# Delta-rule attention, Fourier MLP and token mixing in one Trainium2 kernel: another written-out order of the instruction queues

## The chip, the cores and the metric

One core of one Trainium2 chip runs the whole program. The metric is the device time of an execution in microseconds (us); smaller is better. The kernel before took 953.66 us (median of 3 runs, 952.69 to 954.89).

## The reference

Three steps, each fed by the one before, in float32. A delta-rule attention over 4 batches, 8 heads, 768 positions of width 48; an MLP with a two-dimensional Fourier transform ahead of it; and a token mix with three more weight matrices.

```python
k_n = k / (np.linalg.norm(k, axis=-1, keepdims=True) + 1e-06)
for t in range(S):                                   # attention, state is (B, H, 48, 48)
    y[:, :, t] = einsum('bhd,bhde->bhe', q[:, :, t], state)
    v_old = einsum('bhde,bhd->bhe', state, k_n[:, :, t])
    state = state + beta[:, :, t] * einsum('bhd,bhe->bhde', k_n[:, :, t], v[:, :, t] - v_old)

X = np.fft.fft(np.fft.fft(x, axis=1), axis=2)        # x is y with the heads side by side: (4, 768, 384)
u = x + np.real(X)
un = (u - mean(u)) / np.sqrt(var(u) + 1e-06)
x = u + np.maximum(un @ w_ch1, 0.0) @ w_ch2          # 384 -> 1536 -> 384

theta = x @ w_theta
y = einsum('ts,bsd->btd', w_tok_r, x * cos(theta)) + einsum('ts,bsd->btd', w_tok_i, x * sin(theta))
u = x + y
out = u + np.maximum(u @ w_ch, 0.0)
```

## The kernel before

**Attention.** The 768 positions are cut into 12 windows of 64 per batch; all 48 (4 batches of 12) are scanned in turn. Two windows make a chunk step d (24 of them, 16 pairs of head and window each), and four steps share a solve, T0 to T5. `gram` (L351 to L386) loads keys and queries with the DMA kt, multiplies them on TensorE (PE) into sm and copies the products to KQ. `solve` (L397 to L438) inverts 128 triangular 32x32 blocks on VectorE (DVE): 30 pairs of a product (L434, tmp) and a sum (L437, T), the first pair and the last of 30 elements and the middle ones of 240. `solved` transposes the result twice, into TN (L446) and TT (L448). `chunks` (L509 to L537) makes pa from TN, A on ScalarE (ACT, L518), pt from A and TT, copies TT and pt into YU (L483 or L485, L531), multiplies into pw and copies that to YU (L537). `load` (L493, L495) brings the tiles YQ and Y. `scan` (L549 to L584) is the serial chain from window to window: pu (PE), X (ACT, L555 and L556), ps (PE), X of the next window (ACT, L566 and L567), and py (PE); after every second window a tile y is copied out of py (L581, L583) and stored to ysc (L584). YQ, Y and X have two buffers each, so a load of step d waits until the scans of step d-2 have read them.

**Weights.** They come as 64-bit floats. `Split.steps` turns 128x384 numbers at a time into a high and a low part: a DMA into a raw tile (L239), the magnitude on ACT (L242), the sign on DVE (L243), three more steps there (L244 to L246), the low bits (L249), the high part on ACT (L250), three matmuls that add the pieces up (L251 to L253) and a copy on ACT (L254). There are two raw tiles, so the DMA of one conversion waits for L249 of the last but one. w1 and w2 of the MLP need 24 such conversions, which stand among the attention of batch 0 and 1; those of the token mix (wth, wtr, wti) begin when the last scan has been issued and the attention's buffers are given back.

**Fourier and MLP.** `fourier_inputs` (L610 to L656) folds the six y of a batch with sums and differences on DVE or GpSimd (POOL), two scalings on ACT (L626, L631) among them; `fourier_1` (L671) and `prepare` (L747 to L791) transform and normalise (un, L760); `ffn_up` (L204 to L206, ph; then hh on ACT L802 and hl on DVE L803) and `ffn_down` (L812 to L815, pc) are the MLP. Every product of it is three matmuls, of high and low parts. Then the token mix follows (L1056 to L1136).

**What sets the order.** The Python code writes the instructions down step by step (the string PLAN sets how attention and weights mix). `arrange` then reads the table ORDER: for PE, ACT, DVE and POOL it holds runs "skip+n" over the engine's written instructions (go on by skip, take n), and it chains the instructions in the order so read, so that each of these four queues is fixed to the last instruction. SyncE (SP), which issues nearly all DMAs, is not in the table: the scheduler places its DMAs by what they wait for. The innermost lines:

```python
        for run in runs.split():
            skip, n = run.split("+") if "+" in run else (run, 1)
            at += int(skip)
            queue += w[at:at + int(n)]
            at += int(n)
        for a, b in zip(queue, queue[1:]):
            tc.add_manual_dep(b, a.name, edge, reason="order")
```

Of the kernel before, what the change touches and what calls it, by code (L numbers as in the profile page):

```python
# [80 lines left out]
    "PE": """32+32 -64+32 32+179 111+16 -127+16 56+6 -62+16 70+3 -73+16 162+16 -178+8 49+6 16+16 83+16 -186+16 6+8 8+8 -16+8  # L81
# [46 lines left out]
 63+18 -81+18 27+18 18+18 -81+9 72+63""",  # L128
    "Activation": """0 6+6 -12+2 1+3 -4 9+2 24 -25+2 23 -24+2 46 -25 24 -48+3 46 -47+4 52 -10 -44+13 3 38 -3 -37+2 1 -2 1+2 40+4
# [1130 lines left out]
```

## Time and profile before

| | us |
|---|---|
| median of 3 runs (lowest to highest) | 953.66 (952.69 to 954.89) |
| the profiled execution: its own time | 952.9 |
| its span, first to last instruction | 951.1 |
| PE busy | 877.6 |
| DVE busy | 647.8 |
| ACT busy | 431.3 |
| POOL busy | 304.7 |

The span is what the trace covers; the execution's own time holds 1.8 us more around it. An engine's busy time is the sum over its instructions. The granted clock of TensorE is given as a share of full speed: 0.50 is the lower of its two levels, 1.00 the upper; its mean over the span was 0.930. Names in the rows leave buffer numbers out: w_384ag is w1_0_384ag as well as w1_2_384ag.

### The profile page before, as it was taken

The numbers are of one execution on the slowest core, as the hardware profiler recorded it, in microseconds if no ns is written. First come the engines' busy times: TensorE is split into PE (matmuls) and PEld (weight loads), VectorE is DVE, ScalarE is ACT, GpSimd is POOL, SyncE is SP. The second block draws the span as 40 slices with busy tenths as digits, with TensorE's granted clock in tenths as the row PEclk, the third lists the DMA queues.
The fourth block names the chain that finished last, engine by engine and source line by source line (L and its number), as shares of the span: only waits on it lengthen the run. The fifth ranks groups of instructions, "written<-read, shape, count | busy, mean of one in ns | idle before, by whom it ended". The sixth has DMA issues, their size and how long they took to land.

```text
span 951.1 us, 23435 instructions
## 1 busy us (share of the span) xinstructions
PE 877.6 (92%) x9408; PEld 795.2 (84%) x9408; DVE 647.8 (68%) x1494; ACT 431.3 (45%) x1068; POOL 304.7 (32%) x422
## 2 busy tenths in 40 slices
PE   3688878799999999999999999999998999999998
PEld 3566657678787988888889879998997999999997
DVE  7997889778798962988322588788778844625411
ACT  4357885356453335445324333322574634525300
POOL 3101422231331015314110554555144541534411
PEclk7558975599999999999999999999998999999999
DMA  7413733232421114212021232333023111111001
GB/s 207 149 57 103 222 106 97 86 84 87 128 75 58 35 36 126 68 36 77 27 67 36 84 100 68 100 100 117 17 68 119 49 58 35 50 42 37 22 13 47
DMA packets 42205, 73.58 MB, mean 77 GB/s; under 512 B 6001, under 2 KB 26225, under 8 KB 42097
## 3 DMA queue, kind: packets, MB, share of 16 engines
q1 hardware_dynamic: 41328, 69.72, 24.4%
q0 software_dynamic: 768, 2.36, 0.8%
q8 instruction: 74, 1.21, 0.6%
q14 instruction: 35, 0.28, 0.1%
HBM read 57.91 MB, written 14.16 MB: 76 GB/s over the span
## 4 chain that ended last, share of the span: by engine, by line
PE 71%; DVE 14%; DMA 5%; ACT 5%; issue 3%; SPq 1%; POOL 0%; POOLq 0%; DVEq 0%; ACTq 0%
PE ty L204 5%; PE ty L206 5%; PE ty L205 5%; PE ph L204 5%; PE pc L812 5%; PE pc L815 5%; PE ph L206 4%; PE ph L205 4%; PE pc L813 4%; PE sm L351 3%; PE pw L351 2%; PE py L351 2%; DVE tmp L434 2%; PE pg L671 2%; DVE T L437 2%
## 5 line engine op out<-in xcount | busy, mean ns | idle before, releaser
L204 PE MATMUL ph<-uh,w1h 128*128 128x256 f32 x432 | 125.4, 290 | 3.5 <-DVE un L760 1.6
L206 PE MATMUL ph<-uh,w1l 128*128 128x256 f32 x432 | 121.9, 282 | 0.0
L205 PE MATMUL ph<-ul,w1h 128*128 128x256 f32 x432 | 121.8, 282 | 0.0
L802 ACT ACTIVATE hh<-ph 128x256 fp32r<-128x256 f32 x144 | 55.0, 383 | 139.9 <-PE ph L206 67.4
L803 DVE SCALAR_TENSOR_TENSOR hl<-ph,hh 128x256 fp32r<-128x256 f32 x144 | 60.0, 420 | 77.5 <-ACT hh L802 49.0
L812 PE MATMUL pc<-w2h,hh 128*128 128x384 f32 x288 | 102.4, 356 | 1.2 <-DVE u L818 1.1
L815 PE MATMUL pc<-w2h,hl 128*128 128x384 f32 x288 | 94.6, 356 | 2.9 <-DVE hl L803 2.8
L813 PE MATMUL pc<-w2l,hh 128*128 128x384 f32 x288 | 96.9, 336 | 0.0
L351 PE MATMUL sm<-kt 48*64 48x128 f32 (+1 forms) x896 | 67.7, 312 | 27.4 <-DMA kt<-in_kq_dram 20.9
L204 PEld LDWEIGHTS ph<-uh,w1h 128*128 128x128 f32 x432 | 81.8, 189 | 7.7 <-DVE hl L803 2.8
L497 POOL TENSOR_SCALAR_AFFINE_SELECT YQ<-KQ 64x512 f32<-64x512 f32 x48 | 33.5, 699 | 168.0 <-PE py L351 148.3
L351 PEld LDWEIGHTS sm<-kt 48*64 48x64 f32 x896 | 56.2, 173 | 35.1 <-issue 13.8
L205 PEld LDWEIGHTS ph<-ul,w1h 128*128 128x128 f32 x432 | 81.9, 190 | 0.3
L206 PEld LDWEIGHTS ph<-uh,w1l 128*128 128x128 f32 x432 | 82.0, 190 | 0.0
L434 DVE TENSOR_TENSOR tmp<-T 128x30 f32<-128x30 f32 (+9 forms) x180 | 67.4, 375 | 4.5
L437 DVE TENSOR_TENSOR T<-T,tmp 128x30 f32<-128x30 f32 (+9 forms) x180 | 65.8, 366 | 5.4
L812 PEld LDWEIGHTS pc<-w2h,hh 128*128 128x128 f32 x288 | 54.3, 188 | 6.7 <-issue 1.9
L815 PEld LDWEIGHTS pc<-w2h,hl 128*128 128x128 f32 x288 | 52.4, 188 | 7.2 <-DVE hl L803 4.6
L813 PEld LDWEIGHTS pc<-w2l,hh 128*128 128x128 f32 x288 | 54.3, 189 | 0.1
L1122 POOL TENSOR_TENSOR w2l<-xT,w2h 128x384 fp32r<-128x384 f32 x24 | 25.0, 1045 | 91.6 <-ACT w2h L1121 91.6
L510 POOL TENSOR_TENSOR X<-X,nT 64x384 f32<-64x384 f32 x48 | 41.1, 858 | 37.2 <-DMA X<-in_v_dram 27.5
L1121 ACT ACTIVATE w2h<-xT 128x384 fp32r<-128x384 f32 x24 | 12.5, 524 | 69.5 <-DVE xT L1120 37.3
(307 smaller groups left out, 2297.4 us busy)
## 6 DMA issues: line engine op xcount, KB each, us to landing
kt<-in_kq_dram SPq DMA_DIRECT2D x48, 224.0 KB, 2.7
w_0raw<-in_w_dram SPq DMA_DIRECT2D x15, 384.0 KB, 5.0
YQ<-in_qt_dram SPq DMA_DIRECT2D x48, 96.0 KB, 2.9
X<-in_v_dram SPq DMA_DIRECT2D x48, 96.0 KB, 2.8
Y<-in_kn_dram SPq DMA_DIRECT2D x48, 96.0 KB, 2.6
ysc<-y SPq DMA_DIRECT2D x24, 192.0 KB, 2.2
x2scr<-u SPq DMA_DIRECT2D x12, 384.0 KB
wti_0raw<-in_wti_dram SPq DMA_DIRECT2D x12, 384.0 KB, 3.2
```

The lines of the kernel that those rows point to most:

```text
L204: nc.tensor.matmul(out, lh, rh, start=start, stop=False)
L205: nc.tensor.matmul(out, lh, rl, start=False, stop=False)
L206: nc.tensor.matmul(out, ll, rh, start=False, stop=stop)
L351: self.nc.tensor.matmul(o, l, r, start=True, stop=True, skip_group_check=True)
L434: nc.vector.tensor_tensor(pr, E[:, :, j + 1:, j:j + 1].to_broadcast([P, nb, n, j]), E[:, :, j, 0:j].unsqueeze(2).to_broadcast([P, nb, n, j ...
L437: nc.vector.tensor_tensor(E[:, :, j + 1:, 0:j], E[:, :, j + 1:, 0:j], pr, ALU.add)
L510: nc.gpsimd.tensor_tensor(x[TK[par], par], x[TK[par], par], nT[TK[par], n].unsqueeze(2).to_broadcast([C, 8, D]), ALU.mult)
L802: nc.scalar.activation(hh, ph, AF.Relu)
L803: self.up_end = nc.vector.scalar_tensor_tensor(hl, ph, 0.0, hh, ALU.max, ALU.subtract)
L812: nc.tensor.matmul(self.pc[i], hh[:, i * P:(i + 1) * P], wh, start=(f == 0), stop=False)
L813: nc.tensor.matmul(self.pc[i], hh[:, i * P:(i + 1) * P], wl, start=False, stop=False)
L815: nc.tensor.matmul(self.pc[i], hl[:, i * P:(i + 1) * P], wh, start=False, stop=(f == KF - 1))
```

## The change

Only the four strings of ORDER differ: other runs, and so another order of the same instructions on PE, ACT, DVE and POOL. No instruction is added or removed. SP's order changes too, since its DMAs become ready at other times. The first line of the PE string stands for the rest:

```diff
-    "PE": """32+32 -64+32 32+179 111+16 -127+16 56+6 -62+16 70+3 -73+16 162+16 -178+8 49+6 16+16 83+16 -186+16 6+8 8+8 -16+8
...
+    "PE": """32+32 -48+16 -32+16 48+195 56+3 -27+8 55+16 -111+16 32+8 -16+8 11+3 -46+16 162+16 -148+8 16+3 121+16 -148+8
...
```

In the listings below a name's first number is the window, step or batch, its last a running number; w1_0_384 is the conversion of row block 0, columns 384 to 767, of w1; x8 counts like rows in a run. **First place:** PE after T0, from step 0's pw0 to the first scan matmul pu0. Before:

```order
L351 MATMUL pa2_863<-TN0_572,KQ0_159 32x32 x16
L351 MATMUL pa1_646<-TN0_572,KQ0_159 32x32 x16
L251 MATMUL w1_1_0s_750<-w1_1_0ag_743,ident_61 128x384
L252 MATMUL w1_1_0s_750<-w1l_95,eyes_87 128x384
...
L252 MATMUL w1_2_0s_765<-w1l_95,eyes_87 128x384
L253 MATMUL w1_2_0s_765<-w1h_94,eyes_87 128x384
L351 MATMUL pt1_666<-TT0_574,A1_663 32x32 x16
...
L253 MATMUL w2_0_0s_816<-w2h_96,eyes_87 128x384
L351 MATMUL pw1_689<-YU1_79,Y31_86 48x64 x16
L351 MATMUL pa3_1017<-TN0_572,KQ0_159 32x32 x16
L351 MATMUL pu0_711<-X0_83,YU0_78 64x48 x8
```

Now:

```order
L351 MATMUL pa1_646<-TN0_572,KQ0_159 32x32 x16
L251 MATMUL w1_1_0s_750<-w1_1_0ag_743,ident_61 128x384
...
L351 MATMUL pu0_711<-X0_83,YU0_78 64x48 x8
L351 MATMUL pa2_863<-TN0_572,KQ0_159 32x32 x16
L351 MATMUL pt1_666<-TT0_574,A1_663 32x32 x16
L351 MATMUL py0_733<-X0_83,YQ0_81 64x48 x8
L351 MATMUL ps0_722<-X0_83,Y30_85 48x48 x8
L251 MATMUL w1_2_0s_765<-w1_2_0ag_758,ident_61 128x384
...
L351 MATMUL pw1_689<-YU1_79,Y31_86 48x64 x16
L351 MATMUL pa3_1017<-TN0_572,KQ0_159 32x32 x16
L351 MATMUL pu1_772<-X0_83,YU0_78 64x48 x8
L251 MATMUL w2_0_0s_816<-w2_0_0ag_809,ident_61 128x384
```

pu0 moved ahead of pa2, the conversions w1_2_0 and w2_0_0, pt1, pw1 and pa3, and the second scan's pu1 follows pa3. The conversions w2_1_0 and w2_2_0, which came next before, now stand behind the third scan's matmuls.

**Second place:** SP's queue around the raw tile of w1_0_384. Before, with the X, Y30 and YQ0 of step 2 behind it:

```order
L239 DMA w2_2_0raw_844<-in_w2_dram 128x768
L239 DMA w1_0_384raw_925<-in_w1_dram 128x768
L239 DMA w1_1_384raw_1110<-in_w1_dram 128x768
L493 DMA YQ0_81<-in_qt_dram 48x512 x2
L495 DMA Y30_85<-in_kn_dram 64x384
L509 DMA X0_83<-in_v_dram 64x384
L495 DMA Y30_85<-in_kn_dram 64x384
L509 DMA X0_83<-in_v_dram 64x384
L584 DMA ysc0_708<-y0_0_802 128x384
L239 DMA w1_2_384raw_1125<-in_w1_dram 128x768
```

Now:

```order
L239 DMA w2_2_0raw_844<-in_w2_dram 128x768
L493 DMA YQ0_81<-in_qt_dram 48x512 x2
L495 DMA Y30_85<-in_kn_dram 64x384 x2
L509 DMA X0_83<-in_v_dram 64x384 x2
L584 DMA ysc0_708<-y0_0_802 128x384
L239 DMA w1_0_384raw_925<-in_w1_dram 128x768
L239 DMA w1_1_384raw_1110<-in_w1_dram 128x768
L493 DMA YQ1_82<-in_qt_dram 48x512 x2
L509 DMA X1_84<-in_v_dram 64x384
L239 DMA w1_2_384raw_1125<-in_w1_dram 128x768
L509 DMA X1_84<-in_v_dram 64x384
L495 DMA Y31_86<-in_kn_dram 64x384 x2
```

The two raw tiles of w1_0_384 and w1_1_384 moved behind six loads, all of which wait for scans, and behind the store of y0_0. On DVE the same conversion moved back among the pairs of T1. Before:

```order
L434 TENSOR_TENSOR tmp1_1308<-T1_1285 128x210
L437 TENSOR_TENSOR T1_1285<-T1_1285,tmp1_1308 128x21x10
L243 TENSOR_SCALAR w1_0_384ag_926<-w1_0_384raw_925 128x384
L244 TENSOR_SCALAR w1_0_384ag_926<-w1_0_384ag_926 128x384
L434 TENSOR_TENSOR tmp1_1308<-T1_1285 128x220
L437 TENSOR_TENSOR T1_1285<-T1_1285,tmp1_1308 128x20x11
```

Now:

```order
L434 TENSOR_TENSOR tmp1_1308<-T1_1285 128x210
L437 TENSOR_TENSOR T1_1285<-T1_1285,tmp1_1308 128x21x10
L434 TENSOR_TENSOR tmp1_1308<-T1_1285 128x220
L437 TENSOR_TENSOR T1_1285<-T1_1285,tmp1_1308 128x20x11
...
L434 TENSOR_TENSOR tmp1_1308<-T1_1285 128x240
L249 SCALAR_TENSOR_TENSOR w2l_97<-w2_2_0raw_844,w2_2_0ag_845 128x384
L437 TENSOR_TENSOR T1_1285<-T1_1285,tmp1_1308 128x16x15
L434 TENSOR_TENSOR tmp1_1308<-T1_1285 128x240
L437 TENSOR_TENSOR T1_1285<-T1_1285,tmp1_1308 128x14x17
L434 TENSOR_TENSOR tmp1_1308<-T1_1285 128x234
L243 TENSOR_SCALAR w1_0_384ag_926<-w1_0_384raw_925 128x384
L244 TENSOR_SCALAR w1_0_384ag_926<-w1_0_384ag_926 128x384
```

Seven pairs and the product of an eighth (those of 220, 228, 234, 238, 240, 240, 238 and 234 elements) moved ahead of L243 of w1_0_384. At the ends of T0 and T1, TN (L446) moved ahead of TT (L448); and on ACT the two A copies (L518) now stand ahead of the first copies of TT (L483) there.

**Third place:** SP around the loads Y31 for step 11. Before:

```order
L239 DMA w2_9_0raw_3312<-in_w2_dram 128x768
L239 DMA w2_10_0raw_3327<-in_w2_dram 128x768
L493 DMA YQ1_82<-in_qt_dram 48x512 x2
L584 DMA ysc1_2175<-y1_3_2912 128x384
L509 DMA X1_84<-in_v_dram 64x384 x2
L495 DMA Y31_86<-in_kn_dram 64x384 x2
L239 DMA w2_11_0raw_3342<-in_w2_dram 128x768
```

Now:

```order
L239 DMA w2_9_0raw_3312<-in_w2_dram 128x768
L495 DMA Y31_86<-in_kn_dram 64x384 x2
L239 DMA w2_10_0raw_3327<-in_w2_dram 128x768
L509 DMA X1_84<-in_v_dram 64x384 x2
L493 DMA YQ1_82<-in_qt_dram 48x512
L584 DMA ysc1_2175<-y1_3_2912 128x384
L493 DMA YQ1_82<-in_qt_dram 48x512
L370 DMA kt17_0_0_3111<-in_kq_dram 112x512
L239 DMA w2_11_0raw_3342<-in_w2_dram 128x768
```

The two Y31 loads moved ahead of the X1 loads, the YQ1 loads, the store and a raw tile.

Further on, the scan matmuls of windows 27 to 31 and of 42 to 47 moved ahead of groups of the MLP, and with them the conversions of the token mix's weights on DVE; the MLP's rows between them stand later by what was moved ahead. The matmuls of ph in the MLP's second block of batch 0 (group 6) now follow scan matmuls that stood behind them. From 700 us on, the order changes only among neighbours.

## Rows read from the trace of the kernel before

**Rows 1.** Page: busy us by engine; chain that ended last, by engine.

```profile
PE 877.6 (92%) x9408; PEld 795.2 (84%) x9408; DVE 647.8 (68%) x1494; ACT 431.3 (45%) x1068; POOL 304.7 (32%) x422
...
PE 71%; DVE 14%; DMA 5%; ACT 5%; issue 3%; SPq 1%; POOL 0%; POOLq 0%; DVEq 0%; ACTq 0%
```

**Rows 2.** Windows: length, busy us (instructions) by engine, clock, DMA.

```profile
0.00:52.00 52.00, 28.33 (x360) 24.29 (x362) 43.42 (x110) 20.77 (x49) 10.78 (x29) 0.62 0.61 172
52.00:145.00 93.00, 74.53 (x1256) 57.74 (x1252) 78.81 (x180) 70.32 (x174) 22.36 (x38) 0.81 0.42 123
145.00:160.00 15.00, 14.28 (x288) 12.87 (x288) 13.91 (x37) 8.52 (x23) 2.82 (x4) 0.52 0.17 49
160.00:193.00 33.00, 25.90 (x292) 22.84 (x291) 25.57 (x57) 12.52 (x36) 10.36 (x18) 0.50 0.34 101
193.00:525.00 332.00, 321.87 (x4580) 280.10 (x4579) 224.38 (x573) 155.50 (x419) 84.17 (x149) 0.99 0.23 68
525.00:732.00 207.00, 198.19 (x1396) 184.31 (x1395) 162.15 (x367) 81.89 (x201) 95.74 (x104) 0.98 0.29 87
732.00:951.00 219.00, 214.54 (x1248) 213.01 (x1246) 99.62 (x175) 81.77 (x171) 78.47 (x82) 1.00 0.12 39
```

**Rows 3.** Waits of PE, 0 to 200: total, times, longest.

```profile
PE sm L351 <- DMA kt<-in_kq_dram: 20.2, 12, 7.4
PE pa L351 <- DVE TN L446: 7.1, 2, 4.1
```

**Rows 4.** Waits of DVE, 0 to 200.

```profile
DVE t L610 <- ACT y L631: 6.2, 1, 6.2
...
DVE w_384ag L244 <- ACT w_384ag L242: 3.4, 2, 3.1
DVE w_768ag L243 <- DMA w_768raw<-in_w_dram: 1.9, 2, 1.6
DVE w_384ag L243 <- PE w_384s L253: 1.9, 1, 1.9
```

**Rows 5.** Timeline of PE, 56 to 90: start, length, instruction, idle before.

```profile
57.55 1.07 PE L351 MATMUL pa<-TN,KQ 32*32 32x32 f32 x32 [3.05 <-DVE TN L446]
...
63.27 1.92 PE L351 MATMUL pa<-TN,KQ 32*32 32x32 f32 x64
...
67.20 1.48 PE L251 MATMUL w_0s<-w_0ag,ident 128*128 128x384 f32 x2
...
74.81 0.67 PE L351 MATMUL pu<-X,YU 128*64 128x48 f32 x16
```

**Rows 6.** Timeline of SP's DMA queue, 70 to 92.

```profile
72.83 0.82 SPq L239 DMA_DIRECT2D w_384raw<-in_w_dram  x2
...
86.37 0.54 SPq L584 DMA_DIRECT2D ysc<-y  x1
```

**Rows 7.** Page, groups: busy, mean ns.

```profile
L434 DVE TENSOR_TENSOR tmp<-T 128x30 f32<-128x30 f32 (+9 forms) x180 | 67.4, 375 | 4.5
L437 DVE TENSOR_TENSOR T<-T,tmp 128x30 f32<-128x30 f32 (+9 forms) x180 | 65.8, 366 | 5.4
```

**Rows 8.** Timeline of DVE, 68 to 93.

```profile
76.14 0.35 DVE L243 TENSOR_SCALAR w_384ag<-w_384raw 128x384 uint32<-128x384 uint32 x1
79.60 0.36 DVE L244 TENSOR_SCALAR w_384ag<-w_384ag 128x384 f32<-128x384 f32 x1 [3.11 <-ACT w_384ag L242]
```

**Rows 9.** Timeline of DVE, 112 to 125.

```profile
121.02 1.93 DVE L448 STREAM_TRANSPOSE TT<-T 128x1024 f32<-128x1024 f32 x1
122.80 1.95 DVE L446 STREAM_TRANSPOSE TN<-T 128x1024 f32<-128x1024 f32 x1
```

**Rows 10.** Timeline of ACT, 118 to 135.

```profile
122.99 3.28 ACT L483 ACTIVATE YU<-TT 32x256 f32<-32x256 f32 x8 [0.87 <-DVE TT L448]
```

**Rows 11.** Waits of PE, 200 to 525.

```profile
PE pw L351 <- DMA Y<-in_kn_dram: 1.7, 2, 1.4
...
PE ph L204 <- DVE un L760: 1.0, 1, 1.0
```

More of the change, by code (lines that the diff above doesn't have):

```diff
@@ L80 @@
 ORDER = {
-    "PE": """32+32 -64+32 32+179 111+16 -127+16 56+6 -62+16 70+3 -73+16 162+16 -178+8 49+6 16+16 83+16 -186+16 6+8 8+8 -16+8
[46 rows of a table removed]
- 63+18 -81+18 27+18 18+18 -81+9 72+63""",
-    "Activation": """0 6+6 -12+2 1+3 -4 9+2 24 -25+2 23 -24+2 46 -25 24 -48+3 46 -47+4 52 -10 -44+13 3 38 -3 -37+2 1 -2 1+2 40+4
[22 rows of a table removed]
- -21 1 -2 1+2 16 -13+3 1 -2 9+3 2+2 6 -20 19 -8+2 1 -8 5 5 -5 4 1 -24 21 1 -16 7 -17 23+7""",
-    "DVE": """6 -7 7 6 -15+2 6 -7 6 -4 -4 11 -12 6 -2 1+2 2+7 4 -5+4 1+2 61+5 -66+2 74+3 -77+4 73+2 -75+4 71+2 -73+2 71+3
[25 rows of a table removed]
- -10 14 -6+5 1+3 -18 17+2 -19 18+6 3 -4+3 1+5""",
-    "Pool": """59 -59 15 4 17 8 2 4+2 -55+2 10 -2 -14+2 -4 9+2 1+2 -3 -7+4 29 -21 -2 1+2 1+2 3 -2 1+2 1 -2 -7+2 6+4 4+2 -6+2
[7 rows of a table removed]
- -2 3 5 -3 4 -3 -7 8 -6 -4 5 2+7""",
-    "SP": """4+2 -4+2 19 -24 26 -27 22 -19 21 7+2 -4 -28 27 -5 6 -9 -2 -14+2 4 -15 6 -2 -6 29 -30 30 -31+2 33 -34 4+4 3+2 5+2
[6 rows of a table removed]
- -4 4 6+3 -11 4+2 4 -5 4 3+2 -16+3 13 3 -10+3 7+2 3+3 -12 14 -15+2 3+3 7+2 -6+3 3+9""",
+    "PE": """32+32 -48+16 -32+16 48+195 56+3 -27+8 55+16 -111+16 32+8 -16+8 11+3 -46+16 162+16 -148+8 16+3 121+16 -148+8
[46 rows of a table added]
+ -81+18 27+18 18+18 18+18 -117+9 72+18 18+27""",
+    "Activation": """0 6+6 -9+3 -6+3 35 -27+3 24 24 -25 -26+6 46 -47+4 40 -41+2 50 -10 -42+8 43 -44+3 3 38 -39+8 38+4 -42+4 94 -95+2
[22 rows of a table added]
+ -8 1 -2 6 -14 7 6 -2 1 -25 8 7 -17 23+5 1 -2""",
+    "DVE": """1 14 -2 -6 -6+2 -7 7 -7+3 9 -8 3 -3 3 -2 4+7 4 -5+4 1 1 -2 61 -61+3 58+2 -60 71 -13+2 11 -73+18 55+3 -58+2 57
[25 rows of a table added]
+ 1 1+3""",
+    "Pool": """1 15 4 17 8 2 4 1 -2 -54 -2 11 -2 -13 -2 -3 9+5 -9+4 29 -22+4 1+4 1 -2 1+4 8 -9+2 7 -7 -2 12 -2 3 -2 -14+2 15
[7 rows of a table added]
+ 1 -2""",
+    "SP": """4+2 -4+2 19 -23 22 -9+2 -18 5 27 -5 5+2 -3 -8 -2 1 1 6 -17 -8 -2 -8+2 30 -31+4 28 -29 4 27 -28+3 3+2 5+2 26+2
[6 rows of a table added]
+ -11 4+3 3+2 3 -15 14 -15+2 13 3 -10+3 7+2 3+2 -11 10 3 -15+2 3+3 7+2 -6+3 3+9""",
 }
```

212 rows, old and new, of the table ORDER are left out of this document.

## The prediction, made before the changed kernel ran

> **What bounds the kernel now.** I read the page first, then a table of windows, then the waits of PE and DVE, and last the timelines at the places that the order moves. On the page PE is busy 877.6 of 951.1 us and holds 71% of the chain that ended last, DVE 14% [rows 1]. That is an average over two different stages, and the windows part them [rows 2]. From 193 us on PE is busy 321.87 of 332, 198.19 of 207 and 214.54 of 219 us: a stretch limited by PE's own work, which a new order can't shorten, with 10.1 + 8.8 + 4.5 = 23.4 us of idle time. Ahead of 193 PE is busy 28.33 + 74.53 + 14.28 + 25.90 = 143.0 us and idle for 50; DVE is busy 43.42 + 78.81 + 13.91 + 25.57 = 161.7 and idle for 31.3. There the solves T0 to T2 run on DVE, with the weight conversions among them, and PE waits: 20.2 us for the first loads kt and 7.1 for TN [rows 3]. So ahead of 193 the time is DVE's work up to the end of each solve plus DVE's idle time ahead of it; and the order changes no work there, as the same instructions stand ahead of the ends of T0 and T1 before and after. What can be won in front is DVE's idle time alone. Its named waits: 6.2 us for the scaling L631 of batch 0, 3.4 for the magnitude L242, 1.9 for raw tiles of w1, 1.9 for the matmul L253 [rows 4].
>
> **The change, part by part.** The sum is made against the profiled execution's own 952.9 us, which is 0.76 under the median of the runs shown, 953.66; I add that at the end. A measurement of this kernel can tell about 0.2% (1.9 us) from no change.
>
> *PE after T0.* Ahead of pu0, the matmuls from 67.20 to 74.81 (two conversions, pt1, pw1, pa3) go, 7.6 us, and pa2, half of the 64 matmuls that took 1.92, so 0.9: 8.5 us in all [rows 5]. TN ahead of TT lets pa0 start earlier too, at most by its wait of 3.05 [rows 5]; pt0 needs TT as well, so I take half of that, 1.5. pu0 then starts at 74.8 - 8.5 - 1.5 = 65, in place of 74.81. By itself this gains nothing: nothing of it is on DVE's way to the end of T1. It matters by what waits for the first scans, which is SP.
>
> *SP and the raw tiles.* Before, w1_0_384's DMA was issued at 72.83 and DVE could read it at 76.14, so it landed within 3.3 us [rows 6, 8]. Then DVE stood 3.11 us at L244, for the magnitude on ACT [rows 8]. Now the DMA stands behind six loads that wait for scans and behind the store of y0_0, which was issued at 86.37, 11.6 us after pu0 [rows 5, 6]. From 65 that gives 76.6. But half of what left the front of pu0, about 4 us, now stands between pu0 and y0_0 (two conversions came in, two went out, pt1, pw1 and the two pa came in): the store at about 80.5, the raw tile issued at 81, there at 84.3. On DVE seven and a half pairs moved ahead of L243, at 375 + 366 ns a pair 5.6 us [rows 7], so DVE is ready for it at 76.14 + 5.6 = 81.7. It waits 2.6 us for the tile and then some 0.6 for the magnitude: 3.2 us, against 3.11 before. **Taken: 0.** The ends: all waits on conversions up to T1 go, 3.4 + 1.9 + 1.9 = -7.2 [rows 4]; or the store stays at 86.37, the tile lands at 86.9 + 3.3 = 90.2, DVE waits 8.5 and then the 0.6 for the magnitude, 6.0 more than now.
>
> *TN and TT at T1.* TT took 1.93 us and stood ahead of TN at 121.02, with TN at 122.80 [rows 9]; swapped, pa4 can start 1.9 earlier. But pw4 needs YU, which needs TT, and ACT copied TT in eight pieces for 3.28 us ahead of A [rows 10]. Now A comes first and the pieces after TT, which itself is 1.9 later: what leaves one branch enters the other. Taken 0, between -1.9 and +1.9.
>
> *The folds of batch 0.* DVE's 6.2 us for L631 [rows 4] end with the scaling on ACT, which in both orders follows the last gram copies and copies of X; PE is at the lower clock there with the same matmuls. Taken 0. The ends: the wait goes, -6.2; or the four pairs of T2 that now stand behind the folds are late by 4 times 0.74, +3.0 [rows 7].
>
> *The MLP with attention, from 193.* Only PE's idle time counts, and of it two waits lie where the new order says what changes. pw11 waited 1.7 us for its Y tile [rows 11], whose DMAs stood last of seven behind X loads and a store; now they stand ahead of these, and the scan that frees the buffer is not later: -1.7. The wait of ph for un, 1.0 us [rows 11], stands where scan matmuls of some 0.67 us each (a group of pu, [rows 5]) have moved ahead of ph: two of them cover it, -1.0. The remaining idle time up to 732, 18.9 - 2.7 = 16.2 us, consists of short waits whose neighbours are all shuffled, and I take it to stay as a sum. The ends: half of it goes too, -8.1 more; or the two waits come back elsewhere, 0. The conversions for the token mix, which start earlier, cost nothing: DVE is idle for 332 - 224.38 = 107.6 us of the stretch 193 to 525, so their work has cover there; without it their price would be hl late for pc, which is a wait that PE has already.
>
> *From 732.* Neighbours swapped, 0.
>
> **Sum:** -2.7 us. 952.9 - 2.7 = 950.2 for an execution like the profiled one, 951.0 by the median.
>
> **The clock.** The rows show PE busy for 14.28 of 15 us from 145 to 160 at a granted clock of 0.52, the lower level, and 25.90 of 33 at 0.50 after it; from 193 to 525 it is at 0.99, the upper level, with 321.87 of 332 busy [rows 2]. So a busy PE alone did not bring the upper level there; the small 32- and 64-wide matmuls of attention run in it, and before and after it conversions of 128x384. The Trainium skill (TensorE: Matmul & The Clock Gate, Part 1) says that the default state is throttled and that activity releases the throttle. By that, the stretch from 145 to 160 should have run at the upper level; the trace does not agree. A new order could still meet the release there, and I count that as a rival below.
>
> **Rivals.** (1) *The front wins.* The scans come early enough to free the loads, and the three conversion waits go: -7.2 with -2.7 gives 953.66 - 9.9 = 943.8. For it: 10 us lie between the old and the new start of pu0. Against: the two raw tiles still pace the conversions, as the wait at L253 shows. (2) *Slower: SP's queue holds the raw tile.* The store of y0_0 does not come earlier than before, because its copies on ACT and the first loads are in the way; DVE then stands 6 us more ahead of T1's end, everything behind it starts later, and 193 us becomes 199. Each us that the store comes behind 80.5 is a us of DVE, and 2.7 is won back later; so the rival decides from a store at about 85.1 on (80.5 + 2.7 + 1.9). With the store at 86.37 as before: 953.66 + 6.0 - 2.7 = 957.0, or 959.7 with nothing given back. For it: seven DMAs now stand ahead that wait for another engine each. (3) *Nothing.* The order moves waits only; each of the two that I count returns at a neighbour, and the front is as before: 953.7. For it: PE's stretch from 193 has 97% busy already. (4) *The clock is released in 145 to 193.* PE's matmuls there would need less time, and DVE with 13.91 + 25.57 = 39.5 busy of 48 becomes the bound: -8.5, with -2.7 gives 942.5. Against: the order of PE is nearly the same from T1's end to the folds.
>
> **How the numbers follow.** The forecast 951.0 (949 to 953 with the small ends of its terms) has 0.36, the front's win 0.20, slower 0.18, nothing 0.18, the clock 0.08. Faster by over 0.2%, under 951.8: most of the forecast's case (0.24), the front and the clock, 0.52. Within: the rest of the forecast and nearly all of nothing, 0.29. Slower, over 955.6: 0.19. The range leaves out the clock's lower half and the upper half of the slower case, and some of the front's: 943 to 957.
>
> **What would show it.** In the profile after: pu0 near 65 and the store of y0_0 near 80; DVE's wait at w1_0_384 about 3 us, part of it now on the DMA; the end of T1 (L438) and TN near 121 to 123 as before; L631's wait of 6 us still there; pw without a wait for Y, ph without one for un; DVE with more than 224 us of work between 193 and 525. I am wrong if T1 ends more than 2 us off, if the granted clock between 145 and 193 is not near 0.50, or if PE's idle time after 193 is not 20 to 22 us.

## The result, and the profile after

The changed kernel took **959.03 us** (median of 10 runs, 957.08 to 962.40) and the kernel before 952.82 in 10 runs on the same chip (946.84 to 956.72): a ratio of 1.0086, interval [1.006, 1.0113]. That is slower, by 6.2 us between the medians and 8.2 by the ratio (0.0086 of 953), where 951.0 was forecast, and 959.03 lies outside the range of 943 to 957. The profiled execution took 960.72 us, with a span of 959.0. What the part ahead says of SyncE (SP) has to be mended: its order is written out too, as a fifth string of ORDER (from line 189), and the change rewrites it with the other four; the places shown of SP stand as they are.

The windows of after, with the columns of [rows 2]:

```profile
52.00:145.00 93.00, 74.60 (x1131) 56.62 (x1128) 77.01 (x167) 66.16 (x161) 21.92 (x34) 0.80 0.42 124
145.00:160.00 15.00, 12.44 (x290) 9.83 (x286) 14.05 (x37) 10.01 (x26) 3.85 (x6) 0.88 0.19 56
160.00:193.00 33.00, 25.75 (x452) 22.25 (x447) 27.62 (x69) 17.56 (x49) 10.98 (x25) 0.80 0.36 107
193.00:217.00 24.00, 21.78 (x340) 18.18 (x339) 19.08 (x44) 12.87 (x34) 6.84 (x15) 0.79 0.32 93
193.00:525.00 332.00, 317.53 (x4575) 274.81 (x4573) 227.14 (x575) 156.03 (x421) 86.81 (x146) 0.97 0.23 70
525.00:732.00 207.00, 200.33 (x1358) 186.19 (x1357) 150.01 (x357) 77.93 (x191) 89.03 (x98) 0.99 0.26 78
732.00:959.00 227.00, 221.58 (x1278) 220.13 (x1278) 103.79 (x185) 83.43 (x177) 80.67 (x84) 0.99 0.14 43
```

Against [rows 2]: PE has 332 - 317.53 = 14.5 us of idle time in the stretch from 193, where it had 10.1. Its clock is 0.88 and 0.80 between 145 and 193, where it was 0.52 and 0.50. What PE waited for from 193 to 525 (total, times, longest):

```profile
PE sm L351 <- DMA kt<-in_kq_dram: 2.2, 2, 1.2
PE pw L351 <- ACT YU L531: 1.7, 2, 0.9
PE ph L204 <- DVE u L756: 1.6, 1, 1.6
```

and the same three before:

```profile
PE sm L351 <- DMA kt<-in_kq_dram: 0.7, 1, 0.7
PE pw L351 <- ACT YU L531: 0.5, 2, 0.3
PE ph L204 <- DVE u L756: 0.2, 1, 0.2
```

The waits of [rows 11], pw for its Y tile and ph for un, are gone. In their place pw waits longer for YU, ph for the u that is loaded from ysc, and sm for its kt tiles. DVE's waits from 0 to 210, against [rows 4]:

```profile
DVE s L417 <- ACT s L416: 4.5, 3, 3.7
...
DVE w_384ag L244 <- ACT w_384ag L242: 4.1, 1, 4.1
DVE y L610 <- ACT y L631: 3.5, 1, 3.5
```

The first is new. The timeline of ACT in after shows why:

```profile
64.83 1.21 ACT L537 ACTIVATE YU<-pw 48x512 f32<-48x512 f32 x2 [2.03 <-PE pw L351]
66.07 0.23 ACT L416 ACTIVATE s<-dg 128x32 f32<-128x32 f32 x1
```

and so does DVE's:

```profile
62.46 0.19 DVE L409 COPY dg<-T 128x32 f32<-128x32 f32 x1
66.33 0.18 DVE L417 TENSOR_SCALAR s<-s 128x32 f32<-128x32 f32 x1 [3.68 <-ACT s L416]
```

L416 takes the square root of T1's diagonal. Before, ACT ran it ahead of the two copies YU0<-pw0 (L537):

```profile
61.76 0.23 ACT L416 ACTIVATE s<-dg 128x32 f32<-128x32 f32 x1 [0.41 <-DVE dg L409]
63.38 1.20 ACT L537 ACTIVATE YU<-pw 48x512 f32<-48x512 f32 x2 [1.39 <-PE pw L351]
```

Now it stands behind them, and the copies wait 2.03 us for PE. DVE stands at L417 for 3.68 us. T1 ends with L438, at 126.0 instead of 121.0, before and then after:

```profile
119.77 1.22 DVE L438 TENSOR_TENSOR T<-T,g 128x1024 f32<-128x1024 f32 x1
```

```profile
124.27 1.71 DVE L438 TENSOR_TENSOR T<-T,g 128x1024 f32<-128x1024 f32 x1
```

The expectations below, and the first row of the table, count from the first instruction that does work, 0.3 us behind the zero of the rows shown; there T1 of after ends at 125.7. SP's queue in after, at the place of [rows 6]:

```profile
82.92 0.52 SPq L584 DMA_DIRECT2D ysc<-y  x1
83.54 0.88 SPq L239 DMA_DIRECT2D w_384raw<-in_w_dram  x2
```

**Where the time went.** PE's queue has points ahead of which the same instructions stand in both orders, so the time from one to the next compares like with like. The table gives, in us, the first of them and the lengths of the stretches behind it, named by their times in the kernel before, from PE's records; below it the span and the granted clock of PE from 160 to 193 and from 193 to 217 us of each execution. Labels are those of the experiments.

```
            before after   e1    e2    e3    e4    f1    f2    f3    f5    h1    h2    g1    m1
to 194       194.3 192.7 193.9 192.9 192.0 192.3 191.4 192.8 190.7 192.6 193.9 192.4 192.6 189.0
194 to 244    50.1  51.4  49.0  47.6  49.3  50.8  52.9  52.6  50.8  49.9  50.5  49.1  50.3  55.6
244 to 287    42.6  44.9  44.4  42.1  42.2  44.4  49.3  44.6  43.5  44.2  44.4  43.9  42.1  44.7
287 to 410   122.6 127.5 125.5 126.7 124.9 125.7 127.6 124.5 128.2 123.6 125.0 128.5 123.8 124.4
410 to 465    55.9  57.2  56.8  55.6  55.6  57.5  57.5  57.4  56.0  55.6  55.8  57.7  55.7  57.5
465 to 571   105.0 102.9 102.7 104.4 103.8 103.0 102.6 102.6 103.0 103.0 105.0 104.3 104.8 102.3
571 to 729   158.2 159.7 158.9 157.8 158.3 158.6 158.9 159.4 159.8 159.3 158.0 158.6 157.8 159.6
span         951.1 959.0 953.8 949.3 948.4 955.7 962.7 956.6 954.3 950.6 954.8 956.9 949.4 956.1
clock 160     0.50  0.80  0.62  0.53  0.76  0.52  0.84  0.84  0.55  0.77  0.50  0.52  0.53  0.74
clock 193     0.99  0.79  0.93  1.00  1.00  0.79  0.72  0.72  1.00  1.00  0.86  1.00  0.86  0.57
```

The front ends 1.6 us earlier although T1 ends 5 later. That is less than the scatter of one order: the seven executions with the old front reach the first point between 190.7 and 194.3, and e1 and m1, whose orders are the same up to there, at 193.9 and 189.0. Behind it after loses 1.3 + 2.3 + 4.9 + 1.3 us up to 465, wins 2.1 in the stretch to 571 and loses 1.5 to 729: +9.2 in all, with the last 222 us alike to 0.3. One execution is one draw: the kernel before ran between 942.65 and 958.47 beside the experiments, and in the seven executions with its own order from 287 to 410 that stretch took from 122.6 (before) to 128.2 (f3).

PE's idle time from point to point, the length less its busy time, tells the sources apart. From 244 to 287 it is 0.4 to 0.9 us in the seven executions with the old order there and 2.1 to 5.6 in the seven with the new. From 194 to 244 it is 2.9 to 4.4 in both, and from 410 to 465 it is 0.9 to 1.4 in both, at a clock of 1.00. From 465 to 571 it is 2.3 to 3.5 with the old order and 0.8 to 1.5 with the new.

### The profile page after: what moved, and what is told of

Its sections match the earlier page's. It is cut to its first block, busy times and chain, and to the rows that moved or that the text cites. A ratio compares the mean times of both kernels' runs of the same rounds, so it can differ in the third digit from the quotient of the medians.

```text
span 959.0 us, 23433 instructions
## 1 busy us (share of the span) xinstructions
PE 878.5 (92%) x9408; PEld 793.6 (83%) x9408; DVE 642.4 (67%) x1494; ACT 430.7 (45%) x1068; POOL 304.5 (32%) x422
## 4 chain that ended last, share of the span: by engine, by line
PE 68%; DVE 18%; ACT 5%; DMA 5%; issue 3%; POOL 1%; SPq 0%; POOLq 0%; ACTq 0%; DVEq 0%
PE ty L204 5%; PE ty L206 5%; PE ty L205 5%; PE ph L204 5%; PE pc L812 4%; PE ph L206 4%; PE ph L205 4%; PE pc L815 4%; PE pc L813 4%; DVE T L437 2%; PE sm L351 2%; DVE tmp L434 2%; PE py L351 2%; PE pw L351 2%; PE pg L671 2%
## 5 line engine op out<-in xcount | busy, mean ns | idle before, releaser
L437 DVE TENSOR_TENSOR T<-T,tmp 128x30 f32<-128x30 f32 (+9 forms) x180 | 67.8, 377 | 5.3
L386 POOL COPY KQ<-KQ 32x128 f32<-32x128 f32 x64 | 22.6, 353 | 82.4 <-ACT KQ L384 56.5
```

Source lines behind the costliest of these rows:

```text
L437: nc.vector.tensor_tensor(E[:, :, j + 1:, 0:j], E[:, :, j + 1:, 0:j], pr, ALU.add)
```

## The experiments

All twelve keep every instruction and move some in their queue. **The first theory:** the square root behind the copies makes T1 late, and the end with it. **Its rival:** the front's lateness is taken up before 194 us, and the loss lies behind it, where waits changed places.

**e1_root_back** puts the root where it was (ACT's order of after):

```diff
-ACTIVATE YU0<-pw0 48x512 x2
 ACTIVATE s0_1<-dg_1 128x32
+ACTIVATE YU0<-pw0 48x512 x2
```

> The changed order with one instruction of ACT moved: the square root of T1 (L416) again ahead of the two YU copies of pw0 (L537), behind which the changed order put it. Theory A (the 3.68 us that DVE then stands at L417 is the largest single loss, and it lies on the way to T1's end): DVE's wait at L417 falls from 3.68 us to under 0.5, T1 (L438) ends 3 us or more earlier than 125.7, the time falls by 2.5 to 4 us against the changed kernel, to some 955.5. Rival B (what is won there is lost again at w1_0_384, whose raw tile and magnitude do not come earlier): T1 ends within 1 us of 125.7, and DVE's wait at L244 of w1_0_384 grows from 4.1 to some 7.5.

Measured: 958.77 us in 12 runs, 1.0066 [1.0032, 1.0101] to before. DVE's waits in e1 (this table has other line breaks in the experiments, so lines stand up to 5 lower: L412 is L417):

```profile
DVE y L605 <- ACT y L626: 6.6, 1, 6.6
...
DVE s L412 <- ACT s L411: 1.1, 3, 0.5
```

The root's wait went and T1 ended at 123.3, 2.7 earlier. But the wait for the scaling of the folds (L631 of the kernel before) is 6.6 in place of 3.5: what DVE wins it waits out there. The point at 194 came at 193.9, no earlier than in after. The ratio is 0.0020 under that of after, less than half the width of either interval, so the runs alone don't exclude the 2.5 us of theory A. In m1, with the same order up to there, the wait for the folds was 4.8 us: how much is waited out differs from one execution to the next.

**e2_root_behind** makes the same move alone in the kernel before:

```diff
-ACTIVATE s0_1<-dg_1 128x32
 ACTIVATE YU0<-pw0 48x512 x2
+ACTIVATE s0_1<-dg_1 128x32
```

> The order of before with one instruction of ACT moved: the square root of T1 (L416) behind the two YU copies of pw0 (L537). Theory A: DVE stands 2.5 to 3.5 us at L417 for T1, and the time is 2 to 3.5 us more than before, some 955.5. Rival B: the wait of 3.11 us at L244 of w1_0_384 shrinks by as much, T1 ends within 1 us of before, and the time is within 1 us of before.

Measured: 954.15 us, 1.0021 [0.9986, 1.0055], no difference that 12 runs can tell. ACT in e2:

```profile
63.39 1.19 ACT L532 ACTIVATE YU<-pw 48x512 f32<-48x512 f32 x2 [2.03 <-PE pw L346]
64.60 0.23 ACT L411 ACTIVATE s<-dg 128x32 f32<-128x32 f32 x1
```

The root came 2.84 us later than before (64.60 against 61.76), DVE stood 3.1 us for it, and T1 still ended at 120.8: DVE came later to its next waits, and that for the magnitude at L244 fell from 3.1 to 0.2 us. By this trace the rival holds. The interval of the runs still holds the 2 us of the first theory; that the root is not the whole loss follows from e3, which keeps it late.

What is left: the loss lies behind 193 us, **either** at places of its own, each by waits that took the place of others there, **or** only where the new front meets the new rest, as by the clock.

**e3_front_new and e4_front_old** cut the change in two, by the time at which an instruction starts in the trace of before:

```diff
 ORDER of e3, all five queues
-everything in the order before
+what starts ahead of 193 us: the new order; the rest: the order before
 ORDER of e4
+what starts ahead of 193 us: the order before; the rest: the new order
```

> The new order on all five queues for all instructions that started ahead of 193 us in the trace of before, then the order of before for the rest. If the loss lies in the front (T1 ended 5.0 us later, T2 2.7): 3 to 6 us more than before, 956 to 959. If it lies behind 193 us (PE idle for 14.5 us there up to 525 against 10.1): 0 to 2.5 us more than before.

> The order of before on all five queues for all instructions that started ahead of 193 us in the trace of before, then the new order for the rest. If the loss lies in the front: within 1.5 us of before. If it lies behind 193 us: 3 to 5 us more than before. If the new order behind 193 us wins what the prediction gave it, 2.7 us less than before, 950.

Measured: e3 953.26 us, 1.0016 [0.9983, 1.0049]; e4 954.97, 1.0034 [1.0002, 1.0067]. The new front alone, late root included, changes nothing that can be told (-1.6 to 4.7 us). The new rest alone is slower, by less than the whole change; the intervals are too wide to say whether the two add up to it.

**f1_kt_first** takes the wait for kt away: its DMA goes ahead of the loads it stood behind in SP's order of after.

```diff
+DMA kt17_4_0<-in_kq_dram
 DMA Y30<-in_kn_dram x2
 DMA YQ0<-in_qt_dram
 DMA X0<-in_v_dram x2
-DMA kt17_4_0<-in_kq_dram
```

> The changed order with one DMA of SP moved: the second keys-and-queries tile of window group 17 (kt17_4_0) ahead of the loads Y30, YQ0 and X0 of step 12, behind which the changed order put it. Theory A (SP's queue: the tile's buffer is free, but the DMA stands behind loads that wait for scans): PE's wait of 1.06 us for kt near 254 us falls under 0.3, and the stretch of PE's queue from the conversion w2_10_0 to pc0_1_1's first matmul of hh0_1_0 takes 43.5 us in place of 44.9 (42.1 to 42.6 in the order of before). Rival B (the two sm stand too close together on PE, and the buffer itself is late): the wait stays at 0.8 us or more.

Measured: 964.45 us, one run. The wait went, and the stretch from 244 to 287 took 49.3 us, 4.4 more than in after. SP's queue in f1:

```profile
246.73 0.35 SPq L234 DMA_DIRECT2D w_0raw<-in_w_dram  x1
250.02 0.31 SPq L365 DMA_DIRECT2D kt<-in_kq_dram  x1
250.37 1.61 SPq L490 DMA_DIRECT2D Y<-in_kn_dram  x2
...
259.22 1.57 SPq L692 DMA_DIRECT2D u<-ysc  x1
```

and in after:

```profile
246.64 0.35 SPq L239 DMA_DIRECT2D w_0raw<-in_w_dram  x1
247.04 1.11 SPq L495 DMA_DIRECT2D Y<-in_kn_dram  x2
...
257.66 0.37 SPq L697 DMA_DIRECT2D u<-ysc  x1
```

The kt DMA was held until 250.02, 2.9 us behind the DMA ahead of it, for PE's sm (the second of these two waits of SP, 238 to 262):

```profile
SPq L365 <- PE sm L346: 7.1, 2, 4.2
```

With it everything behind was held: Y30 was issued 3.3 us later than in after and u 1.6 us later. DVE stood for u and PE for DVE (timeline of DVE; waits of PE, 240 to 300):

```profile
267.70 0.56 DVE L751 TENSOR_TENSOR u<-u,pm 128x384 f32<-128x384 f32 x1 [3.63 <-DMA u<-ysc,rows]
```

```profile
PE ph L199 <- DVE u L751: 3.1, 1, 3.1
```

So a dearer wait came in place of the 1.1 us for kt. Not all of it is the queue's: u's issue took 1.57 us in place of 0.37, and DVE got u 8.5 us after that began, where in after 7.0 us were enough. One execution doesn't tell how much of the 4.4 us the move of kt made.

**f2_store_first** takes the wait for u away. In the second block of the MLP of batch 0, u0_2 is complete (L818) at 381.6 + 0.5 us before and at 397.8 + 0.5 in after; its store (L819) is issued 20.3 us later than before (402.45, was 382.16), and the load of u1_1 stands behind it. f2 moves the store ahead of loads:

```diff
+DMA x2scr<-u0_2
 DMA YQ0<-in_qt_dram
 DMA Y30<-in_kn_dram x2
 DMA X0<-in_v_dram
 DMA ysc<-y2_4
 DMA X0<-in_v_dram
 DMA YQ0<-in_qt_dram
-DMA x2scr<-u0_2
 DMA u1_1<-ysc
```

> The changed order with one DMA of SP moved: the store of u0_2 (L819) ahead of the loads YQ0, Y30, X0 and the store of y2_4, behind which it was issued at 402.45 us, 4 us after u0_2 was ready. The load of u1_1 waits for that store, DVE for the load (1.95 us at L753), PE's ph for DVE (1.65 us). Theory A: DVE's wait at that L753 falls under 0.3 us, PE's wait of ph for L756 under 0.5, and the stretch of PE's queue from pc0_1_1's hh0_1_0 to pa19 takes 126 us in place of 127.5 (122.6 to 126.7 in the order of before). Rival B: another wait takes its place, and the stretch stays at 127 us or more.

Measured: 958.35 us, one run. SP's queue in after, then in f2:

```profile
402.45 0.56 SPq L819 DMA_DIRECT2D x2scr<-u  x1
407.12 0.35 SPq L697 DMA_DIRECT2D u<-ysc  x1
```

```profile
399.76 0.56 SPq L814 DMA_DIRECT2D x2scr<-u  x1
...
404.72 0.42 SPq L692 DMA_DIRECT2D u<-ysc  x1
```

The load comes 2.4 us earlier, and these two waits of after are gone, DVE's for the load

```profile
409.63 0.56 DVE L753 TENSOR_TENSOR u<-u,pm 128x384 f32<-128x384 f32 x1 [1.95 <-DMA u<-ysc]
```

and PE's for what DVE makes of it:

```profile
412.24 0.58 PE L204 MATMUL ph<-uh,w1h 128*128 128x256 f32 x1 [1.65 <-DVE u L756]
```

The stretch from 287 to 410 took 124.5 us, and 124.4 in m1, which has this edit too; the five executions with the new order there and without the edit took 125.5 to 128.5. That fits a price of some 2 us for the late store, though the spread within one order is as large.

**f3_middle_new** tries the one stretch that the new order wins, alone; **f5_front_middle_new** adds the new front.

```diff
 ORDER of f3, all five queues
-everything in the order before
+what starts from 465.5 to 570.6 us: the new order; the rest: the order before
 ORDER of f5
+what starts ahead of 193 us, too: the new order
```

> The order of before, and the new order only for the instructions that started between 465.5 and 570.6 us in the trace of before (the last scans, the end of attention). That stretch of PE's queue took 105.0, 104.4 and 103.8 us in three profiles with the old order and 102.9, 102.7 and 103.0 in three with the new. Theory A (what the stretch wins stays won, as PE is the bound from there to the end): 102.7 to 103.0 us for the stretch, and the whole 1 to 2 us under before, 951 to 952, which runs of this number can hardly tell from before. Rival B (it is given back at the token mix's first weights): the stretch as A, but the stretch from pc2_1_0 to the second half of the first ty takes 1 us more than before.

> The new order ahead of 193 us and between 465.5 and 570.6 us, the order of before elsewhere. Theory A (the new front is 3 us late at T2's end and PE's higher clock gives it back by 244 us; the new middle wins 1.5): within 2 us of before, 951 to 953, T1 ends at 124 to 126 and the granted clock from 145 to 193 is 0.7 to 0.85. Rival B (the front's 3 us are lost for good): 954 to 957.

Measured: f3 952.81 us, 0.9986 [0.9959, 1.0014]; f5 954.25, 1.0017 [0.9985, 1.0048]. Both took 103.0 us for the stretch, 2.0 less than before, and both lost 1.6 and 1.1 of it again by 729. A gain of half a us can't be told by runs.

**h1_new_194_287 and h2_new_287_465** ask whether the loss is local to the stretches that lost in the table:

```diff
 ORDER of h1, all five queues
-everything in the order before
+what stands between PE's points at 194 and 287: the new order; the rest: the order before
 ORDER of h2
+what stands between PE's points at 287 and 465: the new order; the rest: the order before
```

> The order of before, and the new order only for the instructions that started between 194.3 and 287.0 us in the trace of before. Theory A (the loss is local, and PE is the bound behind it): PE's two stretches there, up to pa8 to w2_10_0 and on to pc0_1_1, take 51 and 44.5 us (old order 47.6 to 50.1 and 42.1 to 42.6), the stretches behind as before, and the whole is 3 to 4 us over before, 956 to 957. Rival B (made up again behind, as PE has idle time there): the later stretches shrink by as much, the whole within 1.5 us of before.

> The order of before, and the new order only for the instructions that started between 287.0 and 465.5 us in the trace of before. Theory A: PE's stretches from pc0_1_1 to pa19 and on to pc1_1_0's hh1_1_9 take 126 and 57.2 us (old order 122.6 to 126.7 and 55.6 to 55.9), with the late store of u0_2 and DVE's wait at L753 near 410 us in it, and the whole is 2 to 3 us over before, 955 to 956. Rival B: made up behind, the whole within 1.5 us of before.

Measured: h1 957.67 us, 1.0045 [1.0024, 1.0067]; h2 955.66, 1.0029 [1.0004, 1.0053]. Each is slower by itself, on the front before. In h1 the wait of pw for its Y tile is gone as forecast, and others stand there (PE, 190 to 290):

```profile
PE sm L346 <- DMA kt<-in_kq_dram: 1.5, 2, 1.0
PE pu L346 <- ACT X L562: 1.0, 1, 1.0
PE pc L810 <- DVE hl L798: 1.0, 1, 1.0
```

h2 brings back after's wait for u and a longer one for YU (PE, 287 to 465):

```profile
PE pw L348 <- ACT YU L528: 2.6, 1, 2.6
PE ph L201 <- DVE u L753: 1.6, 1, 1.6
```

Its stretch from 410 to 465 took 57.7 us, like the 56.8 to 57.5 of the others with the new order there and unlike the 55.6 to 56.0 of all with the old. So 4.3 + 2.8 us of the loss lie at these two places (the ratios' excess times 953; the intervals are 2.3 to 6.4 and 0.4 to 5.1), against 8.2 of the whole; the front's 1.5 (e3) and the middle's -1.3 (f3) cancel.

**g1_y_first** takes only the forecast's move of Y to the kernel before:

```diff
+DMA Y31<-in_kn_dram x2
 DMA X1<-in_v_dram x2
-DMA Y31<-in_kn_dram x2
```

> The order of before with two DMAs of SP moved: the loads Y31 of step 11 ahead of the X1 loads, as the new order has them. This is the prediction's first late term alone. Theory A (the prediction's): PE's wait of pw11 for Y (1.45 us near 239) goes, the stretch of PE's queue from pa8 to w2_10_0 takes 1 to 1.7 us less, the whole 1.7 us less than before. Rival B (SP's queue: the X1 loads are late in its place, or ACT's copies to YU hold pw11 anyway): the wait for Y goes, another of 0.8 us or more takes its place, the whole within 1 us of before.

Measured: 951.51 us, 0.9970 [0.9938, 1.0001]. It has the lowest median of the kernels that ran in rounds with the kernel before, though the interval holds 1. The wait of pw for Y is gone. In its place PE waits for a kt tile, 1.6 us where it was 0.7 (PE, 190 to 246), as rival B said:

```profile
PE sm L346 <- DMA kt<-in_kq_dram: 1.6, 1, 1.6
```

The stretch took 50.3 us all the same, at a clock of 0.86 in its first part.

**m1_root_and_store** is after with the edits of e1 and f2 together.

> The changed order with two single instructions moved: the square root of T1 ahead of the YU copies of pw0 on ACT, and the store of u0_2 ahead of the step's loads on SP. Theory A (of the changed order's loss only the waits that these two mend are won, the store's 1.5 to 3 us for good, the root's 3 us only up to T2): 956 to 957, some 2 to 3 us under the changed kernel, T1 ends near 123, the stretch from pc0_1_1 to pa19 takes 124 to 125 us. Rival B: both pay in full, 953 to 954.

Measured: 957.76 us, 1.0052 [1.002, 1.0084]. The root's and the store's moves together leave most of the loss, as theory A said. T1 ends at 120.5, T2 at 187.3 (after: 192.1), and the point at 194 is reached at 189.0, 5.3 us ahead of the kernel before and 4.9 ahead of e1, whose order is the same up to there. Its windows:

```profile
160.00:193.00 33.00, 25.14 (x354) 20.82 (x354) 27.01 (x65) 13.66 (x39) 9.60 (x24) 0.74 0.37 98
193.00:217.00 24.00, 22.18 (x283) 19.47 (x284) 13.95 (x37) 12.31 (x32) 7.93 (x15) 0.57 0.30 92
```

and that of the kernel before for the second:

```profile
193.00:217.00 24.00, 21.88 (x398) 18.54 (x397) 16.99 (x44) 14.44 (x39) 9.54 (x22) 0.99 0.39 114
```

m1 ran at the lower clock for most of these 24 us: 283 matmuls in 22.18 us of busy time, against 398 in 21.88 before (not all of them the same ones, as m1 is further on in its order). The stretch from 194 to 244, with the same matmuls, took 55.6 us, 5.5 more than before, and the lead of this execution was spent.

## Why the prediction was wrong

**The step that failed** is "The MLP with attention, from 193": -2.7 us taken, with ends of 8.1 more and of 0. Both waits went as forecast, but nothing was won by it. That the remaining idle time would "stay as a sum" was an assumption, and the end "the two waits come back elsewhere, 0" was set as the worst case, with no reason given why new waits couldn't exceed the old. h1 and h2 give +4.3 and +2.8 us in its place. g1 shows the failure on the first term alone: Y's wait went, and kt's, 0.7 us before, became 1.6 in the same stretch. Rival 3 had named this (each of the two waits "returns at a neighbour"), with the old waits as the most that can return. What the runs show of the sources:

- *Waits that took the places.* kt 2.2 us in all (0.7 before), YU 1.7 (0.5), u 1.6 (0.2). From 244 to 287 they are the loss: with f1 left out, the new order is 1.6 us longer there in the mean and PE idle for 2.3 us more. PE's idle time from 193 was put at 20 to 22 us; it is 14.5 + 6.7 + (227 - 221.58 =) 5.4 = 26.6, where it was 23.4. The rest of the loss is time in which PE is busy for longer.
- *A result that comes later.* Scan matmuls put ahead of the MLP make the MLP's own product late. The prediction saw that as cover for ph; u0_2, 16 us later, and the store and load behind it, it did not follow. f2 shows the chain.
- *Clock.* From 193 to 217 the granted clock is 0.57 to 0.93 in all seven executions with the new order there, and 0.99 or 1.00 in all with the old but g1 (0.86). The stretch from 194 to 244 follows its mean clock, with the same matmuls and as much idle time: 47.6 and 49.3 us at 1.00, 49.0 to 50.8 at 0.96 and 0.97, 50.3 and 50.5 at 0.93, 50.8 and 51.4 at 0.90, 52.6 and 52.9 at 0.87, 55.6 at 0.82. The prediction took the upper level there for granted.
- *PE's own work.* From 410 to 465 the new order costs 1.5 us without more idle time, at a clock of 1.00 in all. The prediction called this work one that "a new order can't shorten"; that it can lengthen it was left out. The cause stays open. More changes from one result tile to another it is not: the new order has 59 there and the old 63.

**Rival 2, slower by SP's queue,** gave the right sign by another place. The store of y0_0 came at 82.92, under its deciding point of 85.1, and DVE's wait at w1_0_384 was 4.1 us where 3.2 was forecast, all of it for the magnitude on ACT and none for the tile. But its mechanism, a queue that holds what stands behind a waiting DMA, is what f1 shows at 250 us: kt held for 2.9 us, and Y30 3.3 us later.

**The front: 0 forecast, 1.0016 measured (e3), by other reasons.** pu0 came at 67.94, where 65 was forecast. That DVE's idle time alone decides in front holds for T1, which ended 5.0 us later and not "near 121 to 123": the square root on ACT, which the rows listed nowhere as a wait, was missed, and it takes 3.4 of the 5.0 (3.68 against 0.3). Of these, 2.7 came back at once: the fixed wait for the folds fell from 6.2 to 3.5, and rose to 6.6 in e1, which has no late root. There that wait was the cover, and the prediction called it unchanged; in m1, also without a late root, it was 4.8, and T2 ended 4.8 us earlier than in after. So the whole front is measured (e3), and how it comes to nothing is shown in single executions only.

**Rival 4, the clock between 145 and 193,** came in full (0.88 and 0.80), at a chance of 0.08, and was worth 1.6 us at 194 at the most, within the scatter of the old front, and not 8.5: PE was quicker there, but T2 ended later (192.1, was 189.4), and PE had to follow it. The reason given against it, the nearly same order of PE, was weak: from 160 to 193 the order decides it in every execution, 0.50 to 0.55 with the old front and 0.62 to 0.84 with the new. From 145 to 160 the old front itself ran from 0.51 to 0.86, so the 0.52 that the prediction built on was one draw.

**The yardstick** was too fine: with runs that spread over 16 us, ten or twelve of them tell 0.3%, not 0.2%.

**Open:** the 1.5 us from 410 to 465, and what in the order sets the clock around 193. The four parts alone make 4.3 + 2.8 + 1.5 - 1.3 = 7.3 of the 8.2 us, each with an interval of 2 us or more to either side, so that a part that comes only from their meeting is not excluded. The coarser cut makes less: 1.5 (e3) and 3.2 (e4) are 4.7.

## What to carry to other kernels

When an order is rewritten, a wait that it removes is worth nothing until you have named who is late next: follow the moved instruction's results (here a store, a load, a normalisation) and what stands behind its waits in the same queue (here a square root behind two copies, and a row of loads behind one kt). In a queue that issues its DMAs in order, an early load that has to wait for its buffer holds what stands behind it (2.9 us in f1). Ask of each lateness whether a fixed wait further on takes it up; and compare two orders at points ahead of which the same instructions stand, in several executions, before one stretch is called won.

## What the runs showed of the hardware

The granted clock is part of an order's price. A busy engine did not bring the upper level: m1 had PE busy for 22.18 of 24 us at 0.57, and the kernel before for 14.28 of 15 us at 0.52 [rows 2], while f3 with the same order up to there had 0.86 in those 15 us at 8.71 us of busy time. With the new front the clock rises between 160 and 193 and is lower from 193 to 217 wherever the new order goes on there, behind the old front too (e4 0.79, h1 0.86); with the old rest behind it (e3, f5) it is 1.00. From 194 to 244 the same matmuls took 47.6 us at a mean clock of 1.00 (e2) and 55.6 at 0.82 (m1): the traced execution of m1 was 5.3 us ahead at 194 and had lost all of it 50 us later.
